# Single-bank output places, weight sums used where they are made, and reordered blocks in a fused attention and mixture-of-depths kernel

## The chip, the cores and the metric

One core of a Trainium2 chip runs the kernel; the other cores are idle. The metric is the device time of one execution in microseconds (us), as a median of several runs. All data are fp32.

## The reference

```python
# q, k, v: (8, 12, 448, 64); x: (8, 448, 768); w1: (768, 1024); w2: (1024, 768)
scores = scale * np.matmul(q, k.transpose(0, 1, 3, 2)) - np.log(S)
attn = 1.0 / (1.0 + np.exp(-scores))
x = np.matmul(attn, v)            # heads joined: (8, 448, 768)
scores = np.einsum('bsd,d->bs', x, w_gate)
out = x.copy()
for b in range(B):
    top_idx = np.argpartition(-scores[b], capacity)[:capacity]   # 128 of 448 rows
    xe = x[b, top_idx]
    ye = np.maximum(xe @ w1, 0.0) @ w2
    g = 1.0 / (1.0 + np.exp(-scores[b, top_idx]))
    out[b, top_idx] = x[b, top_idx] + g[:, None] * ye
```

Attention is sigmoid attention without a softmax. In every batch the 128 rows with the highest gate score go through a two-layer network and are added back.

## The kernel before, in words

**Attention.** Four heads of one batch are a quad; there are 24 quads, two of them in each of twelve steps (`s`, 0 to 11). A step has seven slots (`n`, 0 to 6). In a slot TensorE (PE) multiplies 32 score tiles of K and Q (`score`, L329) into the PSUM tiles `a0` and `a1`, ScalarE (ACT) applies the sigmoid (`squash`, L343), and PE adds attention times values into the tiles `o0` and `o1` (`value`, L358), some slots behind the scores. A tile `a` or `o` is two banks of 512 columns; the four tiles fill PSUM. When a step's values are complete, four slots into the next step, `takes` (L379, VectorE, DVE) transposes the four output banks into the rows of the batch, `gates` (L387, L390) adds up gate scores and, for the last quad of a batch, `gate` puts them into DRAM.

**The network.** For every batch `spread` reads the scores back, copied to all partitions (`rep`, L427, issued by GpSimd, POOL); `ranking` counts on VectorE for each row how many stand above it (L435, L438) and makes a one-hot matrix `hot` (L450); `choose` (L472, L476) turns it into indices on PE; `fetch` evacuates them (`idx`, `got`, L483, L486) and POOL gathers the rows (`xe`, L496). `turn_rows` transposes the gathered rows on PE and evicts two banks into `rows_t`. Two batches are a pair. Pairs are multiplied by a scheme of seven products of quarter matrices, as in Strassen's: `first` (L553, 24 matmuls a product) with the first matrix, `second` (L617, 8 matmuls) with the second; `first_sums` and `second_sums` (L566, L628) evict and combine them on VectorE. `scatter` (L637) writes finished rows back from POOL. The four held or summed quarters of a matrix take 768 KB each: three quarters of each matrix stay on chip (`w1_sb`, `w2_sb`), a fourth is loaded into a spare tile, and `make_sum` (L199) makes four sums for each matrix.

**Order.** The order of every engine's work is written out by hand. `BLOCKS` lists what is done of the network after slot 3 of a step (`after`, L839): ("t", b) turns the rows of batch b, ("c", b) is its choose and fetch, (m, p, key) is a product of pair p with matrix m. `place` in `block` hands out banks of the four two-bank tiles, mostly two to a tile. Before the block come `takes` (in the slot, L751 and L769) and, in steps where a batch is complete (`FULL`) or after it, `gates`. After it come the transposes of Q and K for the next step and the load of the next K, which has one buffer only. `MADE` and `WEIGHTS` say in which slot a sum is made and a quarter is loaded. A sum overwrites a spare tile, so `KEPT` first stores each to DRAM; `LENT` reads sums back one step ahead of their block, up to three of them into the three spare tiles, the last ones into other tiles. `RANKED` says where `ranking` stands.

**Queues.** SP issues nearly all transfers in program order: Q, K, values (`load_v`, L150, right after slot 3 of the step that uses them, from step 5 on), weights, sums, and the stores of finished batches (`store`, four a batch, in two slots of a step and two of the next). POOL issues scores, `rep`, gathers and scatters. After step 11, `rest` finishes the last two pairs.

Of the kernel before, what the change touches and what calls it, by code (L numbers as in the profile page):

```python
# [17 lines left out]
def kernel(  # L18
# [354 lines left out]
    def take(s, pr, x):  # L373

        b, g = divmod(2 * s + x, NG)
        if b not in x_tiles:
# [289 lines left out]
    def do(item, where="any"):  # L666
        t = banks(where)
        if item[0] == "t":
            turn_rows(item[1], t)
        else:  # L670
            finish(item, begin(item, t[:, 0]))

    def block(s):

        free = {name: [0, 1] for name in ("a1", "o0", "a0", "o1")}

        def place(count):
            name = next(x for x in free if len(free[x]) >= count)
            taken, free[name] = free[name][:count], free[name][count:]
            return banks(name) if count == 2 else banks(name)[:, taken[0]]  # L680

        for item in BLOCKS[s]:
# [270 lines left out]
```

## Time and profile before

| what | us |
|---|---|
| median of 3 runs (lowest, highest) | 527.31 (527.19, 529.98) |
| the profiled execution | 530.28 |
| its span, first to last instruction | 528.5 |
| PE busy (share of the span) | 459.6 (87%) |
| DVE busy | 304.9 (58%) |
| ACT busy | 187.4 (35%) |

The profiled execution is one of its own; its span is 1.8 us shorter than its time. A busy PE is not PE at its peak: its clock is at one of two levels, 1.2 and 2.4 GHz, and over the span the granted clock was 0.937 of the higher one. PE's weight loads are shown as PEld, the queues of the engines that issue transfers as SPq and POOLq. Idle time of an engine that others do not wait for costs nothing.

### The profile page before, as it was taken

What the parts mean: (1) busy time and instruction counts of PE and PEld (TensorE: products, weight loads), DVE (VectorE), ACT (ScalarE), POOL (GpSimd) and SP (SyncE); (2) the same over time, 40 slices, a digit from 0 to 9 for tenths busy, and PEclk for the clock granted to TensorE, in tenths of its full rate; (3) what the DMA queues carried; (4) which work ended last, traced back from release to release, by engine and by line L of the source; (5) the groups of instructions that cost most, each with busy time, mean ns of one, the idle gap of its engine ahead of it and who ended that gap; (6) DMA issues with size and microseconds to landing.
All of it is one profiled execution on the core that took longest, in us unless ns stands there. A gap on an engine that the chain in (4) does not pass through costs nothing.

```text
span 528.5 us, 14342 instructions
## 1 busy us (share of the span) xinstructions
PE 459.6 (87%) x6374; PEld 268.3 (51%) x6374; DVE 304.9 (58%) x643; ACT 187.4 (35%) x225; POOL 32.9 (6%) x55
## 2 busy tenths in 40 slices
PE   7999999989417997799997779879989779999995
PEld 3455434334117446444553654644444364967962
DVE  3329465775592584363398257646249528896462
ACT  4666665636301460064064116305505514001000
POOL 6000010010000000000000200000000010102001
PEclk9999999979857898799999799989999969999999
DMA  8977369999931596138984209911997492651001
GB/s 218 260 269 194 140 148 214 235 274 229 369 97 48 171 260 125 31 86 234 200 307 107 77 7 262 227 32 54 239 247 247 135 175 69 166 101 60 31 1 60
DMA packets 115726, 84.67 MB, mean 160 GB/s; under 512 B 90624, under 2 KB 99456, under 8 KB 115664
## 3 DMA queue, kind: packets, MB, share of 16 engines
q1 hardware_dynamic: 113680, 75.84, 54.4%
q0 software_dynamic: 1984, 7.91, 5.1%
q8 instruction: 50, 0.82, 0.7%
q14 instruction: 12, 0.10, 0.1%
HBM read 63.28 MB, written 20.46 MB: 158 GB/s over the span
## 4 chain that ended last, share of the span: by engine, by line
PE 71%; DVE 14%; DMA 9%; issue 3%; ACT 2%; SPq 0%; POOLq 0%; DVEq 0%; ACTq 0%
PE a L329 21%; PE o L358 19%; PE o L553 9%; PE a L617 8%; PE a L553 7%; PE o L617 6%; DMA raw_k<-in_k_dram 3%; DMA spare<-in_moe_w_dram 3%; DVE x_b L379 2%; DMA sum<-spare 2%; DVE xe L628 2%; DVE hidden L566 1%; ACT attn L343 1%; DVE scr L387 1%; DVE scr L438 1%
## 5 line engine op out<-in xcount | busy, mean ns | idle before, releaser
L329 PE MATMUL a<-qT,kT 32*64 32x448 f32 x2624 | 249.5, 543 | 3.0 <-issue 1.4
L343 ACT ACTIVATE attn<-a,bias_s 128x896 f32<-128x896 f32 x162 | 161.9, 1007 | 146.6 <-PE a L329 124.1
L358 PE MATMUL o<-attn,raw_v 32*64 32x448 f32 x2176 | 202.0, 543 | 0.1
L329 PEld LDWEIGHTS a<-qT,kT 32*64 32x64 f32 x2624 | 91.8, 132 | 101.7 <-ACT attn L343 56.8
L358 PEld LDWEIGHTS o<-attn,raw_v 32*64 32x64 f32 x2176 | 75.3, 133 | 37.5 <-issue 30.5
L379 DVE STREAM_TRANSPOSE x_b<-o 128x448 f32<-128x448 f32 x48 | 27.1, 619 | 44.2 <-PE o L358 27.0
L358 PE MATMUL o<-attn,rows_t 32*64 32x448 f32 x448 | 41.3, 537 | 0.0
L311 DVE STREAM_TRANSPOSE kT<-raw_k 128x448 f32<-128x448 f32 x42 | 24.2, 615 | 28.1 <-DMA raw_k<-in_k_dram 16.6
L617 PE MATMUL a<-w_sb,hidden 128*128 128x384 f32 x64 | 26.4, 563 | 5.7 <-DVE got L486 3.3
L390 DVE TENSOR_REDUCE gate_p<-scr 128x14 f32<-128x448 f32 x48 | 29.8, 621 | 1.7
L387 DVE TENSOR_TENSOR scr<-x_b,wg_b 128x448 f32<-128x448 f32 x48 | 29.3, 611 | 1.0
L566 DVE TENSOR_TENSOR hidden<-o,hidden 128x512 f32<-128x512 f32 x16 | 10.7, 688 | 33.0 <-PE o L553 32.9
L569 ACT ACTIVATE hidden<-hidden 128x512 f32<-128x512 f32 x12 | 7.5, 630 | 62.5 <-DVE hidden L566 62.5
L628 DVE SCALAR_TENSOR_TENSOR xe<-a,gate,xe 128x384 f32<-128x384 f32 x30 | 17.1, 611 | 21.2 <-PE a L617 21.0
L303 DVE STREAM_TRANSPOSE qT<-qT 128x896 f32<-128x896 f32 x23 | 25.1, 1090 | 5.2 <-DMA qT<-in_q_dram 5.2
L553 PE MATMUL o<-rows_t,spare 128*128 128x128 f32 x192 | 23.1, 277 | 5.1 <-DVE rows_t L526 2.9
L553 PE MATMUL o<-rows_t,w_sb 128*128 128x128 f32 x168 | 23.8, 307 | 4.3 <-DVE got L486 3.5
L553 PE MATMUL a<-rows_t,w_sb 128*128 128x128 f32 x120 | 18.4, 324 | 9.2 <-DVE got L486 6.6
L553 PEld LDWEIGHTS o<-rows_t,w_sb 128*128 128x128 f32 x168 | 23.0, 222 | 4.8 <-issue 3.6
L553 PEld LDWEIGHTS o<-rows_t,spare 128*128 128x128 f32 x192 | 22.1, 192 | 5.7 <-DVE rows_t L526 3.1
L566 DVE TENSOR_TENSOR hidden<-a,hidden 128x512 f32<-128x512 f32 x16 | 10.7, 687 | 24.1 <-PE a L553 23.9
L553 PE MATMUL a<-rows_t,spare 128*128 128x128 f32 x144 | 20.0, 303 | 4.9 <-DVE rows_t L526 2.9
(115 smaller groups left out, 411.3 us busy)
## 6 DMA issues: line engine op xcount, KB each, us to landing
spare<-sum SPq DMA_DIRECT2D x38, 384.0 KB, 6.6
qT<-in_q_dram SPq DMA_DIRECT2D x24, 448.0 KB, 6.5
out_dram<-x_b SPq DMA_DIRECT2D x32, 336.0 KB, 8.5
raw_k<-in_k_dram SPq DMA_DIRECT2D x22, 448.0 KB, 5.7
raw_v<-in_v_dram SPq DMA_DIRECT2D x36, 224.0 KB, 5.0
sum<-spare SPq DMA_DIRECT2D x8, 768.0 KB, 8.6
w_sb<-in_moe_w_dram SPq DMA_DIRECT2D x6, 768.0 KB, 8.9
rows_t<-in_v_dram SPq DMA_DIRECT2D x8, 224.0 KB, 8.2
```

What stands on the lines that cost most here:

```text
L303: nc.vector.transpose(heads["q", i], heads["q", i])
L311: nc.vector.transpose(kt[:, e], t[:, e].rearrange("p (a n) d -> p n a d", a=2))
L329: nc.tensor.matmul(out[y * Dh:(y + 1) * Dh, h % 2, :S], kt[d, e, r:r + 2].rearrange("d r t -> d (r t)"), qt[d, e], start=(e == 0), stop=(e ...
L343: nc.scalar.activation(a, psc[:, :, :S], AF.Sigmoid, bias=bias_s, scale=QK_SCALE)
L358: nc.tensor.matmul(PO[x][j * Dh:(j + 1) * Dh, pr, :S], raw_v[s][rows, 2 * pr + j, at:at + Dh], attn[s, pr, n][rows, j, :], start=((s, x, p ...
L379: nc.vector.transpose(x_tiles[b][:, :, 2 * g + pr, :], PO[x][:, pr, :S].rearrange("p (r t) -> p r t", t=TT))
L387: nc.vector.tensor_tensor(out=tmp, in0=x_tiles[b][:, :, hp, :], in1=wg_b[:, hp:hp + 1, :].to_broadcast([P, TB, TT]), op=ALU.mult)
L390: nc.vector.tensor_reduce(out=gate_parts[b][:, :, hp], in_=tmp, axis=AX.X, op=ALU.add)
L553: nc.tensor.matmul(ps[:, f, :n], w((t * FH + f) * P, P), x[:, t, :n], start=(t == 0), stop=(t == KH - 1))
L566: nc.vector.tensor_tensor(out=dst, in0=a, in1=b, op=ALU.add)
L617: nc.tensor.matmul(ps[:n, :DH], h[:, t, :n], w(t * DH, DH), start=(t == 0), stop=(t == FH - 1))
L628: nc.vector.scalar_tensor_tensor(out=xe[:n, cols], in0=ps[:n, :DH], scalar=st[b]["gate"][:n, 0:1], in1=xe[:n, cols], op0=ALU.mult, op1=ALU ...
```

## The change

- The output places `o` become four tiles of one bank each; they are opened after slot 2 of step 0, whose scores use the same banks as two tiles before.
- Blocks take single banks from a list, `a1`'s first, the four outputs, and `a0`'s first twice. A leading choose is placed ahead of the takes, its fetch between the takes of the two halves; takes and gates of a full step now stand inside the block.
- Rows are turned at the end of a block; both halves of every turn are evicted apart, one by ACT, one by VectorE.
- Each sum is made into a tile in which the first pair uses it (`lent` is set by `make_sum`); the stores to DRAM stay, the reads for the first pair go. Reads back of 768 KB fall from 24 to 14.
- The first matrix is loaded in steps 2 and 3 in place of 0 and 1, the second in steps 4 to 6 in place of 4; sums are made in steps 4, 6 and 7.
- Batches 0 and 1 are ranked one step earlier, and batch 1's `rep` is read in slot 0 of step 4 instead of slot 3.

```diff
-    tiles = {}
-    for name in ("a1", "a0", "o1", "o0"):
-        pool = ctx.enter_context(tc.tile_pool(name=f"ps_{name}", bufs=1, space=PSUM))
-        tiles[name] = pool.tile([P, 2, 512], F32, name=name)
+    PA = [ps_a.tile([P, 2, 512], F32, name=f"a{n}") for n in range(2)]
+    def open_outs():
+        pool = ctx.enter_context(tc.tile_pool(name="ps_o", bufs=1, space=PSUM))
+        for x in range(2):
+            for pr in range(2):
+                PO[x][pr] = pool.tile([P, 512], F32, name=f"o{x}{pr}")
...
+    def bank():
+        turns[0] += 1
+        return (PA[1][:, 0], PO[0][0], PO[1][0], PA[0][:, 0], PO[0][1], PO[1][1])[turns[0] % 6]
...
     def make_sum(m, key):
-        a, b = room["a"], room["b"]
+        if key == 5:
+            room["a"] = spare(0)
+        elif (m, key) == (1, 6):
+            room["c"] = spare(2)
+        elif m == 2 and key in (4, 6):
+            room["d" if key == 4 else "c"] = spare(key // 4 if key == 4 else 0)
...
+            (1, 5): (a, b, w11, ALU.add), (1, 7): (b, w00, b, ALU.subtract),
+            (1, 6): (c, w11, b, ALU.subtract), (1, 3): (c, wx, c, ALU.subtract),
+            (2, 5): (a, b, w00, ALU.subtract), (2, 7): (b, b, w11, ALU.subtract),
+            (2, 6): (c, w00, b, ALU.subtract), (2, 4): (d, wx, c, ALU.subtract)}[m, key]
         nc.vector.tensor_tensor(out=dst, in0=x, in1=y, op=op)
         sums[m, key] = dst
+        lent[m, key] = [dst[:, pr * QW // 2:(pr + 1) * QW // 2] for pr in range(2)]
...
-    MADE = {(2, 1): (1, 5), (2, 2): (1, 7), (3, 1): (1, 6), (3, 2): (1, 3),
-            (4, 5): (2, 5), (4, 6): (2, 7), (5, 1): (2, 6), (5, 2): (2, 4)}
-    KEPT = {(2, 2): (1, 5), (2, 4): (1, 7), (3, 2): (1, 6), (3, 4): (1, 3),
-            (4, 6): (2, 5), (5, 1): (2, 7), (5, 2): (2, 6), (5, 3): (2, 4)}
-    WEIGHTS = {(0, 6): (1, 0), (1, 1): (1, 2), (1, 2): (1, None), (1, 4): (1, 1),
-            (4, 0): (2, 0), (4, 1): (2, 2), (4, 2): (2, None), (4, 4): (2, 1)}
+    MADE = {(4, 4): (1, 5), (4, 5): (1, 7), (4, 6): (1, 6), (6, 4): (1, 3),
+            (6, 6): (2, 5), (7, 0): (2, 7), (7, 4): (2, 6), (7, 5): (2, 4)}
+    KEPT = {(4, 5): (1, 5), (4, 6): (1, 7), (5, 1): (1, 6), (6, 5): (1, 3),
+            (7, 0): (2, 5), (7, 1): (2, 7), (7, 5): (2, 6), (7, 6): (2, 4)}
+    WEIGHTS = {(2, 6): (1, 0), (3, 1): (1, 1), (3, 2): (1, 2), (3, 4): (1, None),
+               (4, 1): (2, 0), (5, 1): (2, 1), (5, 2): (2, 2), (6, 4): (2, None)}
...
     def join(x):
+        for t in PO[x]:
+            nc.scalar.activation(t[Dh:Dh + 1, S:S + 1], bias_s[Dh:Dh + 1], AF.Copy)
...
-        if not odd:
-            nc.scalar.activation(x[:, 0:2, :, :n], ps[:, :, :KH, :n], AF.Copy)
-        else:
-            nc.scalar.activation(x[:, 2, :, :n], ps[:, 0, :KH, :n], AF.Copy)
-            nc.vector.tensor_copy(x[:, 3, :, :n], ps[:, 1, :KH, :n])
+        nc.scalar.activation(x[:, 2 * odd, :, :n], ps[0][:, :KH, :n], AF.Copy)
+        nc.vector.tensor_copy(x[:, 2 * odd + 1, :, :n], ps[1][:, :KH, :n])
...
-        5: [("t", 0), ("c", 1), (1, 0, 1), (1, 0, 2), ("t", 1), (1, 0, 6)],
-        6: [(1, 0, 7), (1, 0, 4), (1, 0, 5), (1, 0, 3), ("c", 2), (2, 0, 1)],
-        7: [(2, 0, 2), (2, 0, 4), (2, 0, 3), (2, 0, 5), (2, 0, 6), ("t", 2)],
-        8: [(2, 0, 7), ("c", 3), (1, 1, 1), (1, 1, 2), ("t", 3), (1, 1, 6), (1, 1, 7)],
-        9: [(1, 1, 4), (1, 1, 5), (1, 1, 3), ("c", 4), (2, 1, 1), (2, 1, 2), (2, 1, 4)],
-        10: [(2, 1, 3), (2, 1, 5), (2, 1, 6), (2, 1, 7), ("t", 4)],
-        11: [("c", 5), (1, 2, 1), (1, 2, 2), ("t", 5)],
+        5: [("c", 1), ("t", 0), (1, 0, 1), (1, 0, 2), ("t", 1)],
+        6: [(1, 0, 6), (1, 0, 7), (1, 0, 4), (1, 0, 5), (2, 0, 1), ("c", 2)],
+        7: [(1, 0, 3), (2, 0, 2), (2, 0, 5), (2, 0, 7), (2, 0, 3), ("t", 2)],
+        8: [(2, 0, 6), ("c", 3), (2, 0, 4), (1, 1, 1), (1, 1, 2), ("t", 3)],
+        9: [(1, 1, 6), (1, 1, 7), (1, 1, 4), (1, 1, 5), (2, 1, 1), ("c", 4)],
+        10: [(1, 1, 3), (2, 1, 2), (2, 1, 5), (2, 1, 6), (2, 1, 3), ("t", 4)],
+        11: [("c", 5), (2, 1, 4), (2, 1, 7), (1, 2, 1), (1, 2, 2), ("t", 5)],
...
-    LENT = {5: [(1, 6)], 6: [(1, 7), (1, 5), (1, 3)], 7: [(2, 4), (2, 5), (2, 6)],
-            8: [(2, 7), (1, 6), (1, 7)], 9: [(1, 5), (1, 3), (2, 4)],
-            10: [(2, 5), (2, 6), (2, 7)], 11: [(1, 6), (1, 7), (1, 5)]}
+    LENT = {(7, 4): [(1, 6, 2)], (8, 4): [(1, 7, 0), (1, 5, 1)],
+            (9, 4): [(1, 3, 0), (2, 5, 1), (2, 6, 2)], (10, 4): [(2, 7, 1), (1, 6, 2), (1, 7, 0)],
+            (11, 0): [(1, 3, "heads"), (2, 4, "heads")],
+            (11, 6): [(1, 5, "attn"), (2, 5, "heads"), (2, 6, "heads")]}
...
     def block(s):
+        places = [PA[1][:, 0], PO[0][0], PO[0][1], PA[0][:, 0], PO[1][0], PO[1][1], PA[0][:, 0]]
+        work = BLOCKS.get(s, ())
+        if work and work[0][0] == "c":
+            chosen = choose(work[0][1], places.pop(0))
+        takes(s - 1, 0)
+        if work and work[0][0] == "c":
+            fetch(*chosen)
+            work = work[1:]
+        takes(s - 1, 1)
+        if s in FULL:
+            gates(2 * s - 2)
+        for item in work:
...
-            if (s, n) == ((4, 3) if b == 1 else (full, 5 + b % 2)):
+            if (s, n) == ((4, 0) if b == 1 else (full, 5 + b % 2)):
                 spread(b)
...
-    RANKED = [(4, 1), (5, 1), (6, 1), (7, 5), (9, 1), (10, 5), (11, 6)]
+    RANKED = [(3, 1), (4, 1), (6, 1), (7, 5), (9, 1), (10, 5), (11, 6)]
```

## Rows read from the trace of the kernel before

**Rows 1.** Windows: us; busy (count) of PE, PEld, DVE, ACT, POOL; PEclk; DMA share, GB/s

```profile
105.17:112.08 6.91, 4.74 (x64) 2.58 (x52) 6.51 (x18) 2.79 (x5) 0.00 (x0) 0.86 1.02 201
133.62:174.30 40.68, 18.98 (x149) 16.22 (x137) 20.66 (x50) 5.39 (x11) 2.12 (x3) 0.67 0.46 155
193.50:222.71 29.21, 21.94 (x165) 16.71 (x153) 12.22 (x23) 3.99 (x7) 0.99 (x1) 0.83 0.51 117
243.24:262.12 18.88, 17.39 (x103) 9.14 (x91) 5.73 (x10) 2.80 (x5) 0.00 (x0) 1.00 0.92 190
281.46:312.37 30.91, 21.22 (x170) 17.12 (x158) 12.92 (x33) 4.46 (x9) 3.20 (x4) 0.89 0.29 78
331.21:358.27 27.06, 21.93 (x157) 15.00 (x145) 13.74 (x26) 4.00 (x7) 0.99 (x1) 0.94 0.53 122
377.24:394.58 17.34, 14.80 (x94) 7.73 (x83) 6.22 (x12) 2.79 (x5) 1.03 (x1) 1.00 0.95 208
415.92:434.74 18.82, 12.19 (x115) 9.89 (x103) 7.71 (x23) 3.39 (x6) 2.18 (x3) 0.73 0.81 146
174.30:193.50 19.20, 19.20 (x402) 7.59 (x405) 15.13 (x35) 11.53 (x12) 0.00 (x0) 0.98 0.79 225
112.08:117.58 5.50, 5.50 (x66) 2.13 (x73) 2.24 (x4) 1.01 (x1) 1.63 (x2) 0.55 1.01 363
394.58:403.08 8.50, 8.50 (x134) 3.87 (x141) 8.26 (x14) 3.92 (x5) 1.00 (x1) 1.00 1.05 333
```

**Rows 2.** PE's waits: instruction, releaser, us in total, times, longest us

```profile
PE o L476 <- DVE x_b L379: 15.3, 1, 15.3
...
PE a L472 <- DVE xe L628: 5.3, 1, 5.3
PE a L553 <- DVE hidden L566: 4.5, 2, 2.6
```

**Rows 3.** Timeline around block 5: start, us, engine, line, operation [idle before]

```profile
136.71 0.87 PE L514 MATMUL a<-iden,xe 128*128 128x128 f32 x6
...
140.55 1.76 DVE L199 TENSOR_TENSOR spare<-w_sb,spare 128x1536 f32<-128x1536 f32 x1 [6.28 <-DMA sum<-spare]
...
150.48 2.23 DVE L379 STREAM_TRANSPOSE x_b<-o 128x448 f32<-128x448 f32 x4
...
157.94 0.15 DVE L486 COPY got<-o 128x1 f32<-128x1 f32 x1
```

**Rows 4.** Chain that ended last, after the blocks: start, us, what

```profile
462.66 2.68 PE a L553 x24
465.34 2.58 PE o L617 x8
...
481.71 0.66 PE o L514 x6
```

**Rows 5.** Timeline of POOL: scores of batch 1, scatter 0, the gather behind it

```profile
99.29 0.53 POOL L415 DMA_DIRECT2D scores<-total  x1 [29.76 <-DVE by_token L417]
...
292.88 1.02 POOL L637 DMA_INDIRECT out_dram<-xe,idx  x1 [1.58 <-DVE xe L628]
296.75 1.00 POOL L496 DMA_INDIRECT xe<-out_dram,idx  x1 [2.84 <-issue]
```

**Rows 6.** Tile scores, 90 to 120 us: landings of its two transfers (second: rep)

```profile
DMA to landing us min/median/max: 5.4/6.5/7.6
```

**Rows 7.** DMA issues: what, queue, count, KB each, median us to landing

```profile
raw_v<-in_v_dram SPq DMA_DIRECT2D x36, 224.0 KB, 5.0
...
rep<-scores POOLq DMA_DIRECT2D x7, 224.0 KB, 5.2
...
xe<-out_dram,idx POOLq DMA_INDIRECT x7, 5.4
```

**Rows 8.** Values of a step: SP's issue after block 6; PE's weight load after block 10

```profile
254.63 4.21 SPq L150 DMA_DIRECT2D raw_v<-in_v_dram  x4
...
398.54 0.15 PEld L358 LDWEIGHTS o<-attn,raw_v 32*64 32x64 f32 x4 [0.76 <-DMA raw_v<-in_v_dram]
```

More of the change, by code (lines that the diff above doesn't have):

```diff
@@ L239, in weight @@
             halves = lent[m, key]
-            if p != NP - 2:
+            if p != NP - 2 and (m, key, p) not in ((2, 4, 1), (2, 7, 1)):
                 del lent[m, key]
@@ L664, in finish, with do @@
         (first_sums if item[0] == 1 else second_sums)(*args)
-    def do(item, where="any"):
-        t = banks(where)
+    def do(item):
         if item[0] == "t":
-            turn_rows(item[1], t)
+            turn_rows(item[1], (bank(), bank()))
         else:
-            finish(item, begin(item, t[:, 0]))
+            finish(item, begin(item, bank()))
     def block(s):
[L675 to L682, printed above, removed]
+        places = [PA[1][:, 0], PO[0][0], PO[0][1], PA[0][:, 0], PO[1][0], PO[1][1], PA[0][:, 0]]
[10 more added lines that the diff above has]
+        for item in work:
             if item[0] == "t":
-                turn_rows(item[1], place(2))
+                turn_rows(item[1], [places.pop(0) for _ in range(2)])
             elif item[0] == "c":
-                fetch(*choose(item[1], place(1)))
+                fetch(*choose(item[1], places.pop(0)))
             else:
-                finish(item, begin(item, place(1)))
+                finish(item, begin(item, places.pop(0)))
     def ranking(b):
@@ L748, in slot @@
                 squash(s, n, pr, PA[pr])
-            if i == 6:
-                for x in (1, 0):
-                    takes(vs, x)
             return
@@ L767, in slot @@
             squash(s, n, pr, PA[pr])
-            if i == 6:
+            if i == 6 and s not in BLOCKS:
                 takes(vs, half)
@@ L785, in rest @@
         turns[0] = 0
-        shared = banks("any")
-        work = [((1, p, 6), first(p, 6, shared[:, 0]))]
-        chosen = choose(b - 1, shared[:, 1])
-        work.append(((1, p, 7), begin((1, p, 7), banks("any")[:, 0])))
+        work = [((1, p, 6), first(p, 6, bank()))]
+        chosen = choose(b - 1, bank())
+        work.append(((1, p, 7), begin((1, p, 7), bank())))
         gates(2 * NS - 1)
@@ L799, in rest @@
             do((1, p, key))
-        first_sums(*begin((1, p, 3), banks("any")[:, 0]), sums_too=(5, 6))
-        work = {key: begin((2, p, key), banks("any")[:, 0]) for key in (2, 1, 4)}
+        first_sums(*begin((1, p, 3), bank()), sums_too=(5, 6))
+        work = {key: begin((2, p, key), bank()) for key in (2, 1, 4)}
         ranking(b)
-        tile5 = banks("any")
-        work[5] = second(p, 5, tile5[:, 0])
-        chosen = choose(b, tile5[:, 1])
+        work[5] = begin((2, p, 5), bank())
+        chosen = choose(b, bank())
         second_sums(*work[2])
         hidden_sum(p, 7)
-        work[6] = begin((2, p, 6), banks("any")[:, 0])
+        work[6] = begin((2, p, 6), bank())
         fetch(*chosen)
@@ L811, in rest @@
         hidden_sum(p, 3)
-        work[7] = begin((2, p, 7), banks("any")[:, 0])
+        work[7] = begin((2, p, 7), bank())
         for key in (4, 5, 6, 7):
@@ L819, in rest @@
             do(item)
-        work = [((1, p, key), begin((1, p, key), banks("any")[:, 0])) for key in (3, 6, 7)]
+        work = [((1, p, key), begin((1, p, key), bank())) for key in (3, 6, 7)]
         for item, args in work[1:]:
@@ L836, in after @@
                 load_v(s)
-            if odd or s in FULL:
-                gates(2 * s - 2)
             if s in BLOCKS:
                 block(s)
+            elif s in FULL:
+                gates(2 * s - 2)
             if odd and s > 3:
@@ L846, in after @@
             turn("q", 2 * s + 3)
-            if not odd and s not in FULL:
+            if s not in FULL:
                 gates(2 * s - 2)
@@ L907, in stream @@
         turn("q", 0)
+        pool = first_outs.enter_context(tc.tile_pool(name="ps_o", bufs=1, space=PSUM))
+        outs = [pool.tile([P, 2, 512], F32, name=f"p{n}") for n in range(2)]
         for _ in range(3):
-            nc.tensor.matmul(PO[1][:, 0], zero[:, :P], zero, start=True, stop=True)
+            nc.tensor.matmul(outs[1][:, 0], zero[:, :P], zero, start=True, stop=True)
         constants()
```

49 lines of the change are left out of this document (18 added, 31 removed).

## The prediction

> **What bounds the kernel now.** I first read the stretches of the eight blocks. I call a stretch what lies between the start of the scores of slot 3 of a step and the start of slot 4's: slot 3's own 48 products, then the step's block. Outside the blocks TensorE is full: the six slots after block 5 take 19.20 us with PE busy 19.20 [rows 1]. The losses stand in the stretches: block 5 takes 40.68 us with PE busy 18.98 and a granted clock of 0.67, blocks 6, 8 and 11 have clocks of 0.83, 0.89 and 0.73 [rows 1]. Next come PE's waits: one of 15.3 us of L476 for the takes (L379), then waits for the eviction of a sum (xe, L628) and of a hidden part (L566) [rows 2]. The last two are not for operands: L472 multiplies a one-hot matrix, yet waits for the reader of another product. That other product lies in the second bank of the same two-bank tile, so two products in one tile wait for each other's eviction.
>
> Then VectorE around block 5 [rows 3]. PE is ready for the block at 136.71, 3.1 us after its stretch began. VectorE has the weight sum L199 in front, which waits 6.28 us for the store of the sum that it overwrites; a ranking and another sum follow, and the takes start at 150.48. They, two gate parts, a gate and the fetch (two instructions of 0.15) end at 158.09: 7.6 us, 7.3 without the fetch. So block 5 is late because weight sums, made for storing, hold up VectorE.
>
> **What a block must cost.** A first-matrix product takes 2.68 us, a second-matrix one 2.58, turning six columns of rows 0.66 [rows 4]; a choose of eight products, at the 0.11 us of a turn's, about 0.9, one of four 0.4.
>
> **The sum, stretch by stretch.**
>
> Block 4 (6.91 us now [rows 1]) gets worse. Its own choose has no ranking ahead any more, but ranking 1 now stands in step 4, slot 1, ahead of these takes, and it needs the scores of batch 1. They leave POOL at 99.29 [rows 5]; they landed after 5.4 us, the replicated copy (rep) in this traffic after 7.6 [rows 6], at the median after 5.2 [rows 7]. I take 6.5 for rep: it lands at about 111.3. Between the end of the sum at 140.55 (142.31) and the takes at 150.48 stand a ranking and a sum of 1.76, so a ranking takes 6.4 [rows 3]. Ranking to 117.8, two takes of 0.56 and the fetch 0.3: 119.2, plus 0.2 of semaphores. The stretch becomes 14.3: **7.4 lost**, with 5.2 to 7.6 for rep 6 to 9. The slow slot behind it (5.50 at clock 0.55, where three are usual [rows 1]) stays.
>
> The Trainium skill, page "DMA: Bandwidth & Descriptors", section "Anatomy of one DMA", gives 2.0 us plus the bytes at 436 GB/s: an estimate of 2.5 us for rep, by which this loss would be some 4 us smaller. The rows disagree, with 5.2 to 7.6.
>
> Block 5 (40.68). The first matrix is now loaded in steps 2 and 3 and its sums are made in slots 4 to 6 of step 4, 3 x 1.76, 5.3 in all. What hides them: in the six slots after block 5, which hold a ranking, VectorE is busy 15.13 of 19.20 us [rows 1]; the slots after block 4 hold none now, so some 9 of busy time leave room for 5.3. Late there, they would delay these takes as they do now. They are used where they lie. Choose, turn, two products and a turn: 3.1 + 0.9 + 0.7 + 5.4 + 0.7 = 10.8. One new wait: a turn's second half is now copied by VectorE, and that copy stands behind takes and gates: 3.1 + 7.6 + 0.6 (costed as a take) = 11.3 is when the second product can start, instead of 7.4. The stretch ends at 14.7. That wait may bring TensorE's lower level, 1.2 GHz, as the 15.3 us and the shorter waits of block 4 did (clocks 0.67 and 0.86); the slot at 112.08 lost 2.5 us by it [rows 1]. I take 2.0: 16.7, **24.0 won**. The product (1, 0, 6) moves to block 6.
>
> Blocks 6 and 9 (29.21 and 27.06). Four first-matrix products, one of the second and a small choose, each in a bank of its own: 3.1 + 10.7 + 2.6 + 0.4 = 16.8 each. VectorE, without a gate here, is through with takes and gate parts before 10.4, and no bank is used twice, so no eviction holds PE. **12.4 and 10.3 won.**
>
> Block 7 (18.88): 3.1 + 2.7 + 4 x 2.6 + 0.7 = 16.8. But behind it the values wait. SP is one queue: load of K (released by a VectorE transpose after the block), then the weight traffic, two stores, Q and K, two stores, and only then the values of the step. In this step the values' four loads were issued until 258.84 [rows 8]; with the 5.0 that such a load takes [rows 7] from its issue at 258.4, they landed some 40.7 after the block before had ended at 222.71. After the change the steps are 19.2 + 16.8 = 36 us, and this one carries a load and three stores of 768 KB instead of three reads: one more, 3.9 us at the 200 GB/s of these stretches [rows 1]. The values land at 44.6, the slot's second half, 1.5 us in, needs them at 37.5: a wait of 7. **4.9 lost.**
>
> Block 8 (30.91): 3.1 + 2.6 + 0.4 + 2.6 + 5.4 = 14.0 without its turn. VectorE first does takes, gates and gate (10.4), then the sum that releases scatter 0 (11.0). The gather on POOL followed its scatter 3.87 us later [rows 5] and lands 5.4 after that [rows 7]: the turn starts at 20.3, ends at 21.0, and the clock costs 2.5. Stretch 23.5: **7.4 won**.
>
> Block 10 (17.34, and 2.5 more in the two slots behind it, 8.50 for 6.0 [rows 1], where values were late until 398.54 [rows 8]). Now 16.8; the chain of SP starts after VectorE's work as before, 1.5 later, so values land 41.8 after block 9, where 37.5 is wanted: 4.2. **1.2 lost.**
>
> Block 11 (18.82): choose and fetch now ahead of the gates, 3.1 + 0.4 + 5.2 + 5.4 + 0.7 = 14.8: **4.0 won.**
>
> The end: its first product goes to a bank that a take must free (0.56): **0.5 lost**.
>
> Costed at nothing: the second half's copy in other blocks, the second small join on ScalarE (ACT is busy 2.8 of 6.9 us in the stretch of block 4), the new pool of PSUM at slot 3 of step 0, which waits for the same sigmoid as now. Of the four first-matrix loads that move behind stores and Q loads on SP three replace stores of sums; the fourth is 3.9 us of transfers before block 4, within its bound.
>
> Sum: -7.4 + 24.0 + 12.4 - 4.9 + 7.4 + 10.3 - 1.2 + 4.0 - 0.5 = 44.1 us. The profiled execution took 530.28 (span 528.5), which is 3.0 above the median of 527.31; I take the gain off the median: **483**. Bounds of rep, the values' waits and the clock: some 9 either way.
>
> **Rivals.**
> *Transfers are prompt* (0.14). With ten reads of 768 KB fewer, the queue could be short enough that rep and the values come as if alone. Against it: the SP-bound stretches moved 190 to 208 GB/s at DMA shares of 0.92 and 0.95 [rows 1]. Then the 7.4, 7 and 4.2 vanish: 464. By the Trainium skill's formula above, rep, values and sums would all be near this.
> *The places still wait in pairs* (0.13), if the waits [rows 2] come from counting on VectorE and not from tiles. Then blocks 6 and 9 keep their times: 483 + 22.7 = 506.
> *Slower: the values' chain sets every step* (0.04). From block 5's end to block 11's the six steps take 434.74 - 174.30 = 260.4, 43.4 each. Ahead of them 16.6 is won. If the chain from block end to values grew beyond 43.4 + 16.6 / 6 = 46.2 us in each, all would be lost; at 48 the time is 527.3 - 16.6 + 27.6 = 538. For it: 40 us already, and DMA shares above 0.9. Against it: only steps with four stores have it, and bytes fall.
>
> **How the numbers follow.** Forecast 483, chance 0.66, own range 474 to 492; the rest, 0.03, is no change. The range runs from the prompt case, 464, to 500, a blend with the paired one, whose far end it leaves out. Half a per cent is about what a measurement tells from no change: faster 0.93, same 0.03, slower 0.04.
>
> **What would show it.** Right: the 15.3 us wait gone; L199 without a DMA wait ahead of the takes; blocks 6 and 9 near 17 us at clock 1.0 without waits for hidden; a PE wait of near 10 us in block 4 for got, with rep ahead of it; a wait for the gather in block 8; raw_v waits after blocks 7 and 10. Wrong: blocks 6 and 9 over 20 us, a weight sum ahead of takes, or steps of over 40 us between blocks 6 and 10.

## The result, and the profile after

The changed kernel takes **481.91 us** (median of 4 runs, 478.47 to 482.21), the kernel before 528.64 beside it (527.19 to 532.19): ratio 0.909, 95% interval 0.903 to 0.916. The forecast was 483 in 464 to 500. The profiled execution took 481.73 us, with a span of 479.9 where 528.5 was; the mean granted clock rose from 0.937 to 0.973.

The stretches of blocks 4 to 11 after the change, as windows (columns as in [rows 1], where the same stretches of before stand); then the slot behind block 4, the two slots behind block 7 and behind block 10, and the time in which the transfers of steps 3 to 5 run:

```profile
106.13:120.86 14.73, 4.15 (x64) 2.03 (x53) 8.43 (x25) 2.97 (x7) 0.56 (x1) 0.74 0.97 242
142.71:159.27 16.56, 13.12 (x125) 10.28 (x113) 8.17 (x24) 4.15 (x10) 2.13 (x3) 0.90 0.74 209
178.11:194.98 16.87, 16.87 (x164) 14.05 (x152) 9.72 (x18) 4.17 (x9) 0.00 (x0) 1.00 0.45 84
215.68:232.78 17.10, 16.69 (x112) 10.65 (x112) 8.89 (x15) 2.91 (x8) 0.00 (x0) 1.00 0.98 257
252.84:273.63 20.79, 15.73 (x131) 11.41 (x119) 12.63 (x34) 4.63 (x11) 3.31 (x4) 0.92 0.40 105
294.12:310.99 16.87, 16.87 (x165) 13.93 (x153) 9.73 (x18) 4.17 (x9) 0.00 (x0) 1.00 0.66 143
331.87:348.82 16.95, 16.95 (x118) 10.46 (x107) 9.41 (x16) 3.19 (x8) 0.00 (x0) 1.00 0.86 178
370.50:385.80 15.30, 15.03 (x130) 10.95 (x118) 9.27 (x26) 3.53 (x8) 3.16 (x4) 1.00 0.74 141
120.86:126.84 5.98, 5.98 (x64) 2.24 (x72) 5.88 (x10) 1.01 (x1) 1.05 (x1) 0.50 1.21 276
232.78:240.03 7.25, 7.25 (x133) 4.08 (x140) 7.04 (x12) 3.38 (x5) 0.00 (x0) 1.00 0.69 200
348.82:357.69 8.87, 8.47 (x133) 4.22 (x140) 8.56 (x14) 3.38 (x5) 1.03 (x1) 1.00 1.04 327
69.00:157.00 88.00, 70.71 (x1235) 34.59 (x1220) 55.28 (x120) 40.13 (x53) 3.90 (x6) 0.91 0.91 231
```

Read the first number behind each stretch and PE's busy time behind that. Block 5 fell from 40.68 to 16.56, block 6 from 29.21 to 16.87, block 9 from 27.06 to 16.87; in 6, 9 and 10 PE has no gap at all. Block 4 alone got longer, 6.91 to 14.73, with PE's records covering 4.15 of it.

The three longest waits that PE still has for a named releaser (columns as in [rows 2], of which no row is left):

```profile
PE a L338 <- DVE got L495: 10.6, 1, 10.6
PE o L523 <- DMA xe<-out_dram,idx: 5.1, 1, 5.1
PE o L559 <- DVE rows_t L526: 3.4, 1, 3.4
```

They lie in blocks 4, 8 and 5. VectorE around blocks 4 and 5 (timeline; L444 starts the ranking of batch 1, L388 is the takes, L207 a weight sum):

```profile
112.85 0.68 DVE L444 TENSOR_SCALAR_CACHE_REDUCE scr<-rep,who 128x448 f32<-128x448 f32 x1 [5.91 <-DMA rep<-scores]
...
119.52 1.17 DVE L388 STREAM_TRANSPOSE x_b<-o 128x448 f32<-128x448 f32 x2
...
131.73 3.55 DVE L207 TENSOR_TENSOR spare<-w_sb,spare 128x1536 f32<-128x1536 f32 x2
...
145.98 1.18 DVE L388 STREAM_TRANSPOSE x_b<-o 128x448 f32<-128x448 f32 x2 [9.62 <-PE o L367]
```

In block 4 the ranking waits for rep, and the takes stand behind it. Before block 5 it is now VectorE that waits (9.62 us) for PE, where PE waited 15.3 for VectorE in [rows 2, 3]. Two things changed there: VectorE is free at 136.4 (135.20 + 1.16, its last transposes), where its takes could start only at 150.48, and PE comes later, as the stretch of block 5 starts at 142.71 and not at 133.62.

### The profile page after: what moved, and what is told of

Same layout as the page of the kernel before. It is cut to its first block, busy times and chain, and to the rows that moved or that the text cites. A ratio compares the mean times of both kernels' runs of the same rounds, so it can differ in the third digit from the quotient of the medians.

```text
span 479.9 us, 14338 instructions
## 1 busy us (share of the span) xinstructions
PE 447.5 (93%) x6374; PEld 267.4 (56%) x6374; DVE 306.2 (64%) x647; ACT 188.2 (39%) x249; POOL 33.1 (7%) x55
## 4 chain that ended last, share of the span: by engine, by line
PE 83%; DMA 6%; DVE 5%; issue 2%; ACT 2%; SPq 0%; POOLq 0%; DVEq 0%; ACTq 0%
PE a L338 27%; PE o L367 24%; PE o L623 10%; PE o L559 9%; PE a L559 7%; PE a L623 4%; DMA raw_k<-in_k_dram 1%; DMA rep<-scores 1%; ACT attn L352 1%; PE p L914 1%; DMA scores<-total 1%; DVE x_b L388 1%; DMA raw_v<-in_v_dram 1%; DMA xe<-out_dram,idx 1%; ACT hidden L352 1%
## 5 line engine op out<-in xcount | busy, mean ns | idle before, releaser
L338 PE MATMUL a<-qT,kT 32*64 32x448 f32 x2624 | 252.7, 546 | 14.0 <-DVE got L495 10.6
L338 PEld LDWEIGHTS a<-qT,kT 32*64 32x64 f32 x2624 | 98.2, 133 | 106.7 <-ACT attn L352 53.8
L367 PEld LDWEIGHTS o<-attn,raw_v 32*64 32x64 f32 x2176 | 79.6, 133 | 38.3 <-issue 27.8
L388 DVE STREAM_TRANSPOSE x_b<-o 128x448 f32<-128x448 f32 x48 | 27.6, 622 | 54.9 <-PE o L367 42.9
L320 DVE STREAM_TRANSPOSE kT<-raw_k 128x448 f32<-128x448 f32 x42 | 24.2, 613 | 23.9 <-DMA raw_k<-in_k_dram 20.7
L623 PE MATMUL o<-w_sb,hidden 128*128 128x384 f32 x80 | 27.3, 486 | 0.0
L444 DVE TENSOR_SCALAR_CACHE_REDUCE scr<-rep,who 128x448 f32<-128x448 f32 (+1 forms) x32 | 21.5, 673 | 6.8 <-DMA rep<-scores 5.9
L572 DVE TENSOR_TENSOR hidden<-o,hidden 128x512 f32<-128x512 f32 x19 | 12.6, 687 | 19.9 <-PE o L559 19.8
L634 DVE SCALAR_TENSOR_TENSOR xe<-o,gate,xe 128x384 f32<-128x384 f32 x34 | 19.5, 611 | 8.9 <-PE o L623 8.7
L447 DVE SCALAR_TENSOR_TENSOR scr<-rep,who,earlier 128x448 f32<-128x448 f32 (+1 forms) x32 | 21.9, 683 | 1.4
L525 ACT ACTIVATE rows_t<-o 128x384 f32<-128x384 f32 x7 | 3.4, 485 | 48.8 <-PE o L523 48.8
L367 PEld LDWEIGHTS o<-attn,rows_t 32*64 32x64 f32 x448 | 18.3, 131 | 5.2 <-issue 3.9
L559 PEld LDWEIGHTS a<-rows_t,spare 128*128 128x128 f32 x168 | 19.3, 192 | 3.2 <-ACT attn L352 3.2
## 6 DMA issues: line engine op xcount, KB each, us to landing
w_sb<-in_moe_w_dram SPq DMA_DIRECT2D x6, 768.0 KB, 10.7
```

What stands on the lines that cost most here:

```text
L320: nc.vector.transpose(kt[:, e], t[:, e].rearrange("p (a n) d -> p n a d", a=2))
L338: nc.tensor.matmul(out[y * Dh:(y + 1) * Dh, h % 2, :S], kt[d, e, r:r + 2].rearrange("d r t -> d (r t)"), qt[d, e], start=(e == 0), stop=(e ...
L367: nc.tensor.matmul(PO[x][pr][j * Dh:(j + 1) * Dh, :S], raw_v[s][rows, 2 * pr + j, at:at + Dh], attn[s, pr, n][rows, j, :], start=((s, x, p ...
L388: nc.vector.transpose(x_tiles[b][:, :, 2 * g + pr, :], PO[x][pr][:, :S].rearrange("p (r t) -> p r t", t=TT))
L444: nc.vector.tensor_scalar(out=junk[:n], in0=rep[:n], scalar1=own, scalar2=0.0, op0=ALU.is_gt, op1=ALU.add, accum_out=above[:n, c:c + 1])
L447: nc.vector.scalar_tensor_tensor(out=junk[:n], in0=rep[:n], scalar=own, in1=earlier[:n, c, :], op0=ALU.is_equal, op1=ALU.mult, accum_out=l ...
```

## The experiments

All ratios are to the kernel before, run beside each. The first five runs take the change apart, the last four follow the waits that it leaves.

**The change without single banks.**

```diff
         for x in range(2):
+            t = pool.tile([P, 2, 512], F32, name=f"o{x}")
             for pr in range(2):
-                PO[x][pr] = pool.tile([P, 512], F32, name=f"o{x}{pr}")
+                PO[x][pr] = t[:, pr]
```

> The changed kernel, but the four output places are again two tiles of two banks each; order, weights and rankings stay as changed. Theory (two products in one tile wait for each other's eviction): block 6 of the changed kernel puts products 2 and 3 into one tile and product 5 and the choose into another. Its VectorE evicted product 2 at 187.5, where PE had ended it at 186.6, and product 5 at 196.9, where PE had ended it at 194.6: waits of about 1.3 and 2.4, 3.7 in all, and the same in block 9. Blocks 7 and 10 have two such pairs with evictions of 0.6 to 0.8 each, 1.6 a block. Block 11's second product stands behind the gates on VectorE (5 us): about 5.4 and 0.7 for the last turn; block 5 about 1. Sum 18: 500, with 496 to 505 held. First rival (the prediction's price: blocks 6 and 9 lose what they won, 12.4 and 10.3): 505 or more. Second rival (the order of the work on VectorE and not the tiles cleared the waits): under 485, and no PE wait for hidden, xe or got in blocks 6, 9 and 11.

Measured: 511.4 us, ratio 0.966 (0.958 to 0.973), above the range: 29.5 more than the change by the medians. The profiled execution, one of the two fastest of six, has a span of 505.6, 25.7 more than the change's. PE's waits of this run, its stretches of blocks 6 and 11, and the time behind the last block stretch, from step 11, slot 6, on (`rest`):

```profile
PE o L624 <- DVE xe L635: 10.5, 4, 4.1
PE o L624 <- DVE got L496: 6.9, 1, 6.9
PE o L560 <- DVE hidden L573: 5.9, 3, 3.2
PE o L482 <- DVE xe L635: 4.6, 2, 2.3
```

```profile
175.41:196.48 21.07, 17.40 (x164) 13.96 (x152) 11.70 (x21) 4.18 (x9) 0.00 (x0) 1.00 0.30 63
...
376.26:400.03 23.77, 17.93 (x130) 11.99 (x119) 9.59 (x26) 4.31 (x10) 3.15 (x4) 0.86 0.73 140
...
406.10:505.60 99.50, 85.24 (x628) 63.06 (x620) 55.34 (x119) 7.83 (x13) 6.45 (x7) 0.95 0.24 64
```

The same time of the changed kernel:

```profile
391.87:479.90 88.03, 81.13 (x628) 60.50 (x620) 55.85 (x121) 7.79 (x13) 6.45 (x7) 0.99 0.29 73
```

L482 multiplies a one-hot sum and waits for xe, which its product does not read: its neighbour in the tile must be evicted first. So the tile is what is waited for, and my second rival falls. Block 6 loses 4.2 (3.7 expected), block 11 8.5 (6.1): here the evictions stand behind gates, and the clock falls to 0.86, which I had not counted. Against the prediction's price other places pay: 6 and 9 lose 8.4 together and not 22.7; blocks 7, 8 and 10 lose 9.2, of which the slots behind them give back 5.6. The largest part, 11.4 us, lies in `rest` (99.5 for 88.0), which I had not counted at all: PE waits there for xe (3.5) and hidden (3.2), and the clock is 0.95 for 0.99. The kernel before, with its tiles of two banks, lost nothing there (its 87.3 are no more than the change's 88.0): its order of places was made for such tiles, and the changed order is not. So of the 25.7 us some 14 lie ahead of `rest`, where the kernel before had its paired waits.

**Single banks alone.** The kernel before, with the places and joins of the change, the two halves of every turn copied apart (those of even batches both by ACT, as before), and:

```diff
+        places = [PA[1][:, 0], PO[0][0], PO[0][1], PA[0][:, 0], PO[1][0], PO[1][1]] * 2
         for item in BLOCKS[s]:
             if item[0] == "t":
-                turn_rows(item[1], place(2))
+                turn_rows(item[1], [places.pop(0) for _ in range(2)])
```

> The kernel before, with the four output places of one bank each and the changed kernel's cycle of places, but with the old order of blocks, the old rankings and the old weight sums. Theory (a wait for two products of one tile, and nothing else of the change): the waits of L476 for the takes (15.3) and for rows stay; those behind a neighbour in the tile go: in block 5 3.5, block 6 3.3 + 2.6 + 1.4, block 8 5.3, block 9 2.4 + 2.0 + 0.8, block 11 6.6, 27.9 in all, and what the clock lost by them (stretches of 29.21 and 27.06 against 18.7 of products in them: some 8 more). The time is 528 - 36 = 492 if nothing is late in their place; but this kernel still reads ten sums back, and its values landed 40 us after a block, so I expect waits for raw_v to give back some 8: 500, held by 492 to 508. Rival (banks are worth nothing without the new order): over 515.

Measured: 512.2 us, 0.968 (0.958 to 0.978): between the range and the rival, with a gain of some 17. Block 6 did all that was expected, 16.99 for 29.21, block 9 fell to 20.26. What took the rest shows in PE's waits and in the stretches of blocks 5 and 8:

```profile
PE o L517 <- DVE x_b L382: 16.0, 1, 16.0
PE o L517 <- DMA xe<-out_dram,idx: 8.2, 2, 7.6
PE a L517 <- DMA xe<-out_dram,idx: 6.5, 1, 6.5
PE o L361 <- DMA raw_v<-in_v_dram: 3.0, 1, 3.0
```

```profile
135.75:172.23 36.48, 18.11 (x148) 15.20 (x136) 21.19 (x50) 5.66 (x14) 2.12 (x3) 0.72 0.53 173
...
266.77:296.98 30.21, 20.94 (x171) 17.42 (x159) 12.18 (x31) 4.75 (x11) 3.19 (x4) 0.83 0.30 80
```

Freed of the paired waits, PE runs into the turns (L517) before their rows are gathered. Block 8 gains 0.7, though its wait of 5.3 is gone.

**The old weight sums in the changed kernel.** The old `MADE`, `KEPT`, `WEIGHTS`, `make_sum` and `load_left`, and

```diff
-    LENT = {(7, 4): [(1, 6, 2)], (8, 4): [(1, 7, 0), (1, 5, 1)],
+    LENT = {(5, 4): [(1, 6, 0), (1, 7, 1), (1, 5, 2)], (6, 4): [(1, 3, 0), (2, 5, 1), (2, 7, 2)],
+            (7, 4): [(2, 6, 0), (2, 4, 1), (1, 6, 2)], (8, 4): [(1, 7, 0), (1, 5, 1)],
```

> The changed kernel, but the weights are loaded, summed and stored in the old slots, and the first pair reads every sum back from memory; banks, order and rankings stay as changed. Theory (a sum that must wait for the store of the one that it overwrites stands ahead of the takes of block 5): the wait of 6 us of the sum comes back, without the ranking behind it; the last sum ends some 3 to 5 us after the takes could start (145.9 in the changed kernel), and the clock costs 1 to 2. The seven reads of 768 KB more make the values of steps 6 to 8 late by 2 to 3 us each. Time 482 + 5 + 7 = 494, held by 487 to 501. Rival (only the ranking made block 5 late; the sums fit where they were): block 5 within 1 us of 16.6, and the time under 486.

Measured: 480.1 us, 0.905 (0.898 to 0.912), the same as the change: the rival. Block 5 takes 17.65. VectorE ahead of it (timeline; L202 is the last sum, L382 the takes):

```profile
144.77 1.76 DVE L202 TENSOR_TENSOR spare<-w_sb,spare 128x1536 f32<-128x1536 f32 x1 [5.68 <-DMA sum<-spare]
146.62 1.18 DVE L382 STREAM_TRANSPOSE x_b<-o 128x448 f32<-128x448 f32 x2
```

The sum waits for the store as it did in [rows 3], 5.68 for 6.28 us. It ends at 146.53, just when PE lets the takes begin (some 3.3 after the stretch's start at 143.35). That is 10.2 later than VectorE was free in the change, and it costs nothing because PE comes so late: the block 4 of this run waits for rep too. That wait also takes up what the old sums cost before it (slot 4 of step 3 takes 6.74 for 3.18, block 4 then 13.46 for 14.73). So in this kernel the new place of the sums and of the weight loads is worth nothing that these runs can tell, and the reads more (eight, by the issues in the two traces, and not seven) cost nothing that they can tell. Where block 4 does not wait it may be otherwise: that was not run (see the lighter run below).

**The rankings alone.** The kernel before, with

```diff
-    RANKED = [(4, 1), (5, 1), (6, 1), (7, 5), (9, 1), (10, 5), (11, 6)]
+    RANKED = [(3, 1), (4, 1), (6, 1), (7, 5), (9, 1), (10, 5), (11, 6)]
-            if (s, n) == ((4, 3) if b == 1 else (full, 5 + b % 2)):
+            if (s, n) == ((4, 0) if b == 1 else (full, 5 + b % 2)):
```

> The kernel before with the rankings of batches 0 and 1 alone moved as in the change (from step 4, slot 1 and step 5, slot 1 to step 3, slot 1 and step 4, slot 1; the copy rep of batch 1 with them); weight sums, places and blocks are the old ones. Theory after the run with the sums read back (the ranking, and not the sums, made block 5 late): the wait of 15.3 for the takes goes. Block 5 is then takes, gates and fetch to 10.9 after its start, two products of 5.4, the gather's landing at about 16.5, a turn, the last product at 21.5 and some 3 of clock: 24.5 where 40.7 was. Block 4 takes on the wait for rep, 14.5 where 6.9 was. Time 528 - 16 + 7.5 = 519, held by 514 to 524. Rival (the prediction's reading: the weight sums, made for storing, hold up VectorE): block 5 stays above 33, and the time is 527 or more.

Measured: 526.0 us, 0.990 (0.986 to 0.994): beyond the range, short of the rival. VectorE ahead of block 5 (timeline), PE's wait there, and the block's stretch:

```profile
141.91 1.76 DVE L199 TENSOR_TENSOR spare<-w_sb,spare 128x1536 f32<-128x1536 f32 x1 [7.65 <-DMA sum<-spare]
147.16 1.76 DVE L199 TENSOR_TENSOR spare<-w_sb,spare 128x1536 f32<-128x1536 f32 x1 [3.49 <-DMA sum<-spare]
148.83 2.23 DVE L379 STREAM_TRANSPOSE x_b<-o 128x448 f32<-128x448 f32 x4
```

```profile
PE o L476 <- DVE x_b L379: 4.6, 1, 4.6
```

```profile
142.24:173.01 30.77, 19.59 (x152) 16.69 (x137) 13.52 (x30) 5.77 (x11) 2.13 (x3) 0.72 0.35 110
```

The wait falls by 10.7 us, but not because VectorE is that much sooner. The takes start at 148.83, where they started at 150.48 [rows 3]: 1.65 earlier without a ranking of 6.4. The sums, which wait 7.65 and 3.49 for the stores of those that they overwrite, hold VectorE almost as long as before; the ranking had stood in what is now the second of these waits. What moved is PE: block 4 takes 9.58 for 6.91 and slot 4 of step 3 8.20 for 3.67, so that the stretch of block 5 starts 8.6 later, at 142.24 for 133.62. It takes 30.77 for 40.68 and ends at 173.01 for 174.30. So neither theory's time came true, and the rival's cause stands: with the ranking or without it, the sums set to within 1.65 us when these takes can start. The 10.7 that the expectation of the next run puts down to the ranking are for the most part PE's later arrival.

**Banks and rankings, old order.** The second and the fourth run's edits together.

> The kernel before with single banks and the changed cycle of places, and with the two rankings moved: what is left to the run with the sums read back (480) is the new order in the blocks alone, with the takes and the fetch set into it. Theory (the order is a part of its own: it puts a step's turn, which waits for a gather, behind as many products as there are): block 5 falls from the 36.5 of the run with banks alone to about 26, since the ranking's share of the wait for the takes was 10.7 in the run with the rankings alone; blocks 4 and step 3, slot 4 take on the 7 that they took on there; the waits for the gathers of blocks 8 and 11 (7.6 and 6.5) stay. Time 512 - 10.5 + 7 = 508, held by 502 to 513, so that the order is worth some 28. Rival (banks and rankings together are the change, the order only fits them): 490 or less.

Measured: 508.9 us, 0.957 (0.949 to 0.964), 0.9 from the expectation. The order of the blocks, with takes, fetch and gates set into it, is worth the 29 us to the run with the old sums. (With the order also go the slots in which sums are read back, and the copy of an even turn's second half on VectorE; they were not taken apart.) PE's waits for gathers that the old order leaves:

```profile
PE o L517 <- DMA xe<-out_dram,idx: 8.9, 2, 7.6
PE a L517 <- DMA xe<-out_dram,idx: 6.2, 1, 6.2
```

| kernel | us | ratio |
|---|---|---|
| rankings alone | 526.0 | 0.990 |
| banks alone | 512.2 | 0.968 |
| all but the banks | 511.4 | 0.966 |
| banks and rankings | 508.9 | 0.957 |
| and the order (old sums) | 480.1 | 0.905 |
| and the sums: the change | 481.9 | 0.909 |

**The wait in block 4.**

```diff
-    RANKED = [(3, 1), (4, 1), (6, 1), (7, 5), (9, 1), (10, 5), (11, 6)]
+    RANKED = [(3, 1), (4, 4), (6, 1), (7, 5), (9, 1), (10, 5), (11, 6)]
```

> The changed kernel with one edit: the ranking of batch 1 stands in step 4, slot 4, behind block 4, and not in slot 1. Theory (block 4 waits only because the takes stand behind a ranking whose input has not landed): PE's wait of 10.6 for got goes, the stretch of block 4 falls from 14.7 to between 4.7 and 7, the slot behind it from 6.0 to near 3.1. VectorE then has takes, transposes, gate parts, a sum, the ranking of 6.6 and two sums behind block 4, some 24 us from 109, to 133, and is needed for the takes of block 5 at about 135: no new wait there. Time 482 - 12 = 470, held by 468 to 474. Rival (the transfers of steps 3 to 5, with DMA shares of 0.94 to 1.08 between 100 and 130, set the pace, and what PE saves it loses by a wait for raw_v, kT or qT before block 6): 478 or more, with such a wait of 5 us or more.

Measured: 484.8 us, 0.912 (0.904 to 0.920): the rival. Windows of this run: block 4, slot 0 of step 5, slot 4 of step 5; then VectorE's wait behind block 4 (timeline) and PE's waits:

```profile
107.54:112.14 4.60, 4.15 (x65) 2.03 (x53) 1.34 (x5) 2.97 (x7) 0.00 (x0) 1.00 1.03 275
122.42:132.25 9.83, 5.75 (x65) 3.10 (x73) 6.76 (x11) 1.22 (x2) 0.00 (x0) 0.65 0.84 187
156.90:167.31 10.41, 6.42 (x66) 2.44 (x66) 8.17 (x14) 2.11 (x4) 0.58 (x1) 0.84 1.03 196
```

```profile
121.16 1.11 DVE L312 STREAM_TRANSPOSE qT<-qT 128x896 f32<-128x896 f32 x1 [7.99 <-DMA qT<-in_q_dram]
```

```profile
PE a L338 <- DVE qT L312: 5.1, 2, 4.1
PE o L367 <- DMA raw_v<-in_v_dram: 4.0, 1, 4.0
```

Block 4 falls by 10.1 and the slot behind it by 2.9, as expected; the slots at 122 and 157 lose 6.8 and 7.4, because Q and the values have not landed. The wait of 10.6 us is the largest of the changed kernel, and taking it away alone wins nothing: in a time of 88 us with a DMA share of 0.91 it covered transfers that are late anyway.

**Fewer transfers there.**

```diff
-    WEIGHTS = {(2, 6): (1, 0), (3, 1): (1, 1), (3, 2): (1, 2), (3, 4): (1, None),
-               (4, 1): (2, 0), (5, 1): (2, 1), (5, 2): (2, 2), (6, 4): (2, None)}
+    WEIGHTS = {(1, 6): (1, 0), (2, 0): (1, 1), (2, 1): (1, 2), (2, 2): (1, None),
+               (5, 4): (2, 0), (5, 6): (2, 2), (6, 4): (2, None), (6, 5): (2, 1)}
...
                 block(s)
+                if s == 4:
+                    ranking(1)
...
-    RANKED = [(3, 1), (4, 1), (6, 1), (7, 5), (9, 1), (10, 5), (11, 6)]
+    RANKED = [(3, 1), None, (6, 1), (7, 5), (9, 1), (10, 5), (11, 6)]
```

> The changed kernel with the ranking of batch 1 directly behind block 4, and with the weight loads moved out of the time in which the transfers are full: the four of the first matrix from steps 2 and 3 to between 44 and 57 us, where SP issues none, and the three of the second from between 116 and 153 to behind block 5. Theory (steps 3 to 5 are bound by transfers, so that a wait of PE in block 4 only covers them): with 5.5 MB fewer between 69 and 157 the wait of 10.6 in block 4 goes (14.7 + 6.0 become 4.6 + 3.1) and does not come back in step 5, slots 0 and 4, where the run with the late ranking lost 6.8 and 7.4; slot 2 of step 3 falls from 6.7 to about 4. Time 482 - 13 - 2.5 = 467, held by 463 to 472. Rival (the stores of rows and the order on the SP queue, which stay, set the pace and not the bytes): the waits for qT and raw_v come back, 477 or more.

Measured: 475.8 us, 0.898 (0.893 to 0.903), between the two. Windows: block 4, slot 4 of step 7, and the transfers' time; then the takes of block 5 (VectorE's timeline):

```profile
105.22:109.82 4.60, 4.15 (x64) 2.03 (x53) 1.34 (x5) 2.97 (x7) 0.00 (x0) 1.00 0.92 249
221.83:231.71 9.88, 6.16 (x66) 3.00 (x65) 9.60 (x15) 1.37 (x3) 0.00 (x0) 0.83 1.00 242
69.00:157.00 88.00, 81.55 (x1428) 41.76 (x1420) 63.25 (x133) 45.27 (x61) 4.27 (x6) 0.94 0.75 178
```

```profile
133.99 1.18 DVE L388 STREAM_TRANSPOSE x_b<-o 128x448 f32<-128x448 f32 x2 [2.07 <-PE o L367]
```

With a DMA share of 0.75 for 0.91 block 4 and slots 0 and 4 of step 5 take 4.60, 4.61 and 3.06: block 6 starts 10.7 earlier than in the change (167.44 for 178.11). Then slot 4 of step 7 takes 9.88 for 3.67: it waits for values (3.7 us of PE's waits are for raw_v). The load that I moved to step 6, slot 5 is one more ahead of them on SP's queue; that it is the cause was not tested alone. Here PE is ready for the takes of block 5 at 133.99. The old sums kept VectorE until 146.5 in the run that had them in the changed kernel, so in this one they could cost up to 12 us: an estimate, as no run has both, and with fewer transfers their stores may land sooner.

**The three smaller waits.**

```diff
-        nc.vector.tensor_copy(x[:, 2 * odd + 1, :, :n], ps[1][:, :KH, :n])
+        if odd:
+            nc.vector.tensor_copy(x[:, 3, :, :n], ps[1][:, :KH, :n])
+        else:
+            nc.scalar.activation(x[:, 1, :, :n], ps[1][:, :KH, :n], AF.Copy)
...
-        if s in FULL:
+        if s in FULL and s != 8:
             gates(2 * s - 2)
-        for item in work:
+        for i, item in enumerate(work):
+            if s == 8 and i == 1:
+                gates(2 * s - 2)
...
-            for a, at in enumerate(((full, 5), (full, 6), (full + 1, 1), (full + 1, 2))):
-            for a, at in enumerate(((full, 5), (full, 6), (full + 1, 1), (full + 1, 2))):
+            for a, at in enumerate(((full, 5), (full, 6), (full + 1, 3 if b % 2 else 1), (full + 1, 3 if b % 2 else 2))):
```

> The changed kernel with three edits that lie in different stretches: both halves of the turns of even batches are copied by ScalarE (block 5); in block 8 the gates stand behind the sum that releases scatter 0; the last two stores of batches 3 and 5 stand behind the load of the values (blocks 7 and 10). Theory (each of the waits that are left is what the prediction named): block 5 loses the wait of 3.4 for rows_t and its clock, 16.6 becomes 11.5 to 12; but the values of step 5, which landed at 156.5, are then wanted at 156 and cost some 1; block 8 has its gather 5 us earlier, at 16 after its start, 20.8 becomes 16.5, and the slot behind it 4.7 becomes 3.1; the slots behind blocks 7 and 10 (3.7 + 3.6 and 5.2 + 3.7) become 3.1 + 3.1. Time 482 - 4 - 6 - 3.5 = 468.5, held by 464 to 474. Rival (the transfers set the pace of all steps): the waits turn up as waits for raw_v, kT or qT, 477 or more.

Measured: 473.6 us, 0.890 (0.884 to 0.896), in the range. Windows of blocks 5 and 8, of the two slots behind blocks 7 and 10, and of the slot behind block 5:

```profile
141.70:156.32 14.62, 11.46 (x125) 8.64 (x113) 7.83 (x23) 5.44 (x13) 1.54 (x2) 1.00 0.79 225
250.66:268.69 18.03, 15.05 (x131) 11.18 (x119) 13.22 (x36) 4.31 (x10) 2.71 (x4) 1.00 0.49 130
231.82:237.88 6.06, 6.06 (x129) 2.71 (x136) 5.92 (x10) 3.77 (x6) 0.00 (x0) 1.00 0.52 117
343.76:349.82 6.06, 6.06 (x129) 2.71 (x136) 5.92 (x10) 3.76 (x6) 1.03 (x1) 1.00 0.97 248
...
156.32:161.07 4.75, 4.75 (x65) 1.92 (x72) 4.61 (x9) 1.43 (x3) 0.58 (x1) 0.64 0.23 53
```

The slots behind blocks 7 and 10 have lost their waits (6.06 for 7.25 and 8.87). Block 8 won 2.8 of the 4.3 expected, block 5 1.9 of 5: in each a turn waits 3 us for its gather, in block 5 in place of the wait that went. What block 5 won is given back at once: the slot behind it takes 4.75 us, at a granted clock of 0.64, where it took 3.06. So the time lies in the range mostly by the other two edits. A fourth buffer for gathered rows, which would let the gather of block 8 go ahead of scatter 0, was not tried.

**All of these.** The last two runs' edits together.

> The edits of the two runs before it (late ranking with early and late weight loads; the three small ones) together. Theory (two separate causes, in different stretches): the gains add up, 482 - 15.5 - 13.5 = 453, held by 450 to 460. Rival (both gains are the same slack of the transfers): no better than the better one of the two by more than 3.

Measured: **464.4 us**, 0.875 (0.871 to 0.879), which beats the change by some 17. That is above the range, which was reckoned from the gains expected of the two runs and not from those found, and far better than the rival. The gains found alone were 6.1 and 8.3; together they are 17.5, which fits the trace: the values of step 7, which the lighter run waited for, now stand ahead of the stores, and slots 4 and 5 of step 7 take 6.06. Blocks 4 and 5 take 4.60 and 15.99.

## Why the prediction was right

**Single banks: mechanism right, price too simple.** The waits of [rows 2] for a neighbour in the tile were read rightly: blocks 6 and 9 came to 16.87 where 16.8 was forecast. But 22.7 us are neither what the banks alone give (17) nor what they are worth to the change (25.7 by spans, 11.4 of it in `rest`), and all the rest of the change without them brought block 6 to 21.07. The rival that the places still wait in pairs is excluded by both runs. The Trainium skill, page "Perfetto Trace Analysis", section "Matmul Optimizations", asks that all eight banks be used. Before and after use all eight here; these runs add that it also matters whether two of them are one tile.

**Block 5: size right (16.7, measured 16.56), cause right as far as it goes.** The prediction said that weight sums, made for storing, hold up VectorE. The run with the rankings alone bears this out: without a ranking the takes still start at 148.83, behind sums that wait for stores; in the changed kernel, with the sums moved, VectorE is free at 136.4. What the prediction did not see is that its terms for blocks 4 and 5 hang together. The wait that the ranking brings into block 4 makes PE 9 us later at block 5, and at that time even the old sums would have been done: put back, they cost the block 1.1 us. How the 15.3 us would divide with PE as early as before, no run shows. The new wait for the turn's second half was there, 3.4 for the 3.9 forecast, and the clock's 0.90 cost some 1.7 (an estimate: a tenth of the stretch), near the 2.0.

**Block 4: right as it stands (14.3, measured 14.73; rep 6.3 for 6.5), wrong as a loss.** That the chain of rep and ranking holds the takes is shown. But it was not 7.4 that another order alone would have kept: without it the transfers take the time elsewhere. With weight loads moved as well, block 6 starts 10.7 earlier.

**Values.** The wait behind block 7 was the term that was most mis-sized: 7 forecast, 1.2 measured (7.25 for the two slots' 6.06). The values landed 40.45 after block 6's end, as before the change (40.7 by the prediction's reading) and not at the 44.6 forecast: the transfer more did not show at the end of the chain. And the slots between took 20.7 for 19.2, so that PE came later. Behind block 10 it was 2.8 for 4.2. That SP's order is the cause is shown by the run with three edits.

**Block 8.** 20.79 and 1.6 in the slot behind it, 22.4 for 23.5; the gather waited for scatter 0 as forecast. **Block 11:** 15.30 for 14.8.

By profiled spans the gain is 528.5 - 479.9 = 48.6, 4.5 over the sum of 44.1: the values give 7.2 and block 8 1.1, and about 4 go back in blocks 4 and 11 and in slots around them (slot 2 of step 3 took 6.69 for 5.19). By the medians beside each other it is 46.7, 2.6 over; the kernel before came out 1.3 above the median from which the gain was taken. So it is partly luck that 483 and 481.9 lie so close: the errors of the terms, and this one, have both signs.

Of the other rivals, prompt transfers fell by the 6.3 of rep. The Trainium skill's formula (page "DMA: Bandwidth & Descriptors", section "Anatomy of one DMA") gives an estimate of 2.5 for it, with which the trace does not agree. The values' chain did not set the steps: the six from block 5's end to block 11's took 37.8 each (385.80 - 159.27), where 46.2 would have eaten the gain.

## What to carry to other kernels

Here an instruction waits for the last reader of a *tile*, so two results that are evicted at different times belong in two tiles. Where several waits end close together, no part of a change has a price of its own: the banks were worth 17 us alone and 29.5 with the rest (by the medians), the order 29 once banks and rankings were done; take parts out and put them in before believing a term. A wait also gets shorter when the engine that waits comes later: compare the times at which the releaser is done, not the lengths of the wait, before naming a cause. And the longest wait of the bottleneck engine may only cover transfers: look at the DMA share around it before paying to remove it.

## What was not expected of the hardware

SP's own issue of a transfer can take long. One store of finished rows (L405) took SP 0.58 to 7.36 us to issue, with a median of 0.84 over 32 of them; what sets it no run here takes apart. In the changed kernel, before the values of step 7 (SP's timeline):

```profile
219.04 7.78 SPq L405 DMA_DIRECT2D out_dram<-x_b  x2
226.91 3.94 SPq L153 DMA_DIRECT2D raw_v<-in_v_dram  x4
```

Two stores hold SP for 7.78 us before it can issue the loads behind them. In the last run, which has the values ahead of these stores, the same issue began at 212.78, 6.2 after block 7 began, and not 11.2. Most of these 5 us were lost again on the way: each load took 9.1 to 10.0 us from its issue to its landing, where it took 4.2 to 5.6 in the changed kernel, so the last one landed 18.4 after block 7 began and not 19.8, just enough for the wait of 1.2 behind block 7, which went.
